# Pairing the attention pieces' y products in one PSUM bank, in a state-space and two-layer kernel ordered by a planner

## The chip, the cores and the metric

The kernel runs on one core of a Trainium2 chip. The metric is the device time of one execution in microseconds. The engines are called as in the profile: PE (TensorE; PEld is its weight load), DVE (VectorE), ACT (ScalarE), POOL (GpSimd), SP (SyncE, which issues most DMAs).

## The reference

A chunked state-space layer feeds two dense blocks. The layer has 4 batches, 8 heads, 768 steps, head size 32 and state size 16. Only this of it matters:

```python
for c in range(nc):
    L = np.exp(cum[:, :, :, None] - cum[:, :, None, :]) * causal
    M = np.einsum('bhin,bhjn->bhij', Cc, Bc) * L
    y[:, :, sl] = M @ xc + (Cc @ state) * decay_to_i
    state = decay_full * state + sum_j(Bx * decay_from_j)
x = y.transpose(0, 2, 1, 3).reshape(3072, 256)
h = x @ w_in;  g = h * sigmoid(1.702 * h);  x = g @ w_out
h = x @ w2_in; g = h * clip(h + 3, 0, 6) / 6;  out = g @ w2_out
```

Both dense blocks have width 256, inner width 2048 and 3072 tokens. All is fp32, and nearly fp32 accuracy is kept.

## The kernel before

**Order.** Every instruction group is added to a planner (class `Schedule`) with an engine, a guessed duration, a key (a due time) and the buffers that it reads, writes or takes anew. The planner simulates the engines, picks on each the earliest possible group and among equals the smallest key, and so fixes the order of each engine's queue before anything is built. Keys and guessed durations set only this order; on the chip the engines run their queues in order and wait on semaphores.

**Attention.** The layer is cut into 32 pieces q: 8 chunks of 96 steps, 4 batches each (`q = 4c + b`). A piece needs decay matrices `l:q` (two scans on DVE, line 425; for q of 6 and more the source is loaded by a DMA into one of 4 buffers), then S = B C products with the state columns appended (`s_mm`, line 460; from q = 6 on for two pieces at a time, in the banks `s`, `y` and two `acc`), then a multiplication of S by decay for each half of the heads (`g_mul` on DVE, line 463, or `g_copy` on ACT and `g_pool` on POOL, lines 466 and 470; `GMP` chooses), and then the y products (`y_mm`, line 481): 8 products of 112 rows by 32 columns, in the trace two records each. `YBANK(q)` puts even pieces in bank `y` and odd ones in bank `s`. ACT copies the new state out (`y_state`, line 485) and y as a rounded high half (`y_out`, line 495); DVE takes the low half (`y_lo`, line 498) and transposes the states of two batches (line 502) for the next chunk. `PIECE(q)` gives a piece's key.

**Dense blocks.** A fp32 product is made of three products of fp32r halves: high by low, high by high, low by high. The 3072 token columns are 6 blocks of 512. In the first dense block, blocks k = 0 to 3 go unit by unit (k, m), m = 0 to 15: 6 products of the first layer (`l1`, line 600), gelu on ACT (603), high half on ACT (612), low half on DVE or POOL (615; `GLP` chooses), and two units later 6 products of the second layer (`l2`, line 625). Blocks 4 and 5 and all of the second dense block (called A4, B0, B2, B4) go two blocks at a time with seven first-layer products in place of eight (`product`, line 761), whose parts ACT copies (`p_copy`, 770) and DVE adds (`p_add`, 773). Block k starts when all its columns are there; block 1 is columns 512 to 1023, pieces 5 to 10.

**Weights.** They come as 64-bit words and are unpacked (ACT line 332; ACT 337 or DVE 339, chosen by `LOW`), joined on DVE (343), rounded to a high half on ACT (346, `TOP`) and a low half on POOL (350). Weights 0 to 15 belong to the first dense block and are due unit by unit in block 0; 16 to 31 are decoded during A4 and B0.

**Outputs.** `outs` scales the sums of the second dense block by 1/6, half the features on ACT (line 778) and half on DVE (780), into one of 3 `gg` buffers, and SP stores each in two DMAs (783). The last sums are those of blocks 4 and 5.

Of the kernel before, what the change touches and what calls it, by code (L numbers as in the profile page):

```python
# [22 lines left out]
CH = 96  # L23
# [29 lines left out]
SKEY = lambda kind, i, lead, t: lead - 52 + 7 * i if i < NS_BX else t - 14  # L53
OPK = lambda kind, k, lead: [lead - 30 + 3.5 * i for i in range(7)] if kind == "A" else [lead - x for x in (22, 20, 18, 14, 9, 7, 5)]
GLQ = lambda kind, j: j == 1 or (kind == "B" and j == 0)
DECODE = (("A", 4), 14.0, 7.5)
# [8 lines left out]
def YBANK(q):  # L65
    return f"{'ys'[q % 2]}:y{q}"


PK = (48, 4, 88, 5, 114, 7, 156, 5)
UGAP = (4, 0.45)  # L70


def PIECE(q):
    if q < 6:
        return 6 + 2.2 * q + 3 * (q > 3)
    if q < 11:
        return PK[0] + PK[1] * (q - 6)
    if q < 16:
        return PK[2] + PK[3] * (q - 11)
    if q < 22:  # L80
        return PK[4] + PK[5] * (q - 16)
    return PK[6] + PK[7] * (q - 22)

# [140 lines left out]
def ssd_moe_kernel(ctx: ExitStack, tc: tile.TileContext, xs, aa, bc, bcz_d, bc0, wu, pat, idn, out):  # L224
# [247 lines left out]
    def y_view(q):  # L472
        return B_(YBANK(q))[:, 0:2 * E].rearrange("p (g e) -> p g e", g=2)

    def y_mm(q):
        c, b = divmod(q, NB)
        yv, x = y_view(q), B_(f"xs:{c}")
        for g in range(2):
            for k in range(4):
                h = 4 * g + k  # L480
                nc.tensor.matmul(out=yv[32 * k:32 * k + 32, g, :], lhsT=x[0:E, b, h * D:(h + 1) * D],  # L481
                                 rhs=B_(f"gm:{q}.{g}")[:, k, :], start=True, stop=True)

    def y_state(q):
        nc.scalar.copy(st_sb[:, q % NB, :, 0:NS], y_view(q)[:, :, CH:E])
# [8 lines left out]
    def y_out(q, k, a, b):  # L494
        nc.scalar.copy(x_part("h", q, k, a, b), y_view(q)[:, :, a:b])

    def y_lo(q, k, a, b):
        nc.vector.tensor_tensor(out=x_part("l", q, k, a, b), in0=y_view(q)[:, :, a:b], in1=x_part("h", q, k, a, b).bitcast(F32), op=ALU.subtract)
# [15 lines left out]
    for q in range(NC * NB):  # L514
# [40 lines left out]
        add("PE", 0.62, t + 2, y_mm, q, r=[f"gm:{q}.0", f"gm:{q}.1", f"xs:{c}"] + [f"xs:{c}.{b // 2}.{k}" for k in range(4) if c], new=[yn])  # L555
        if c + 1 < NC:
            add("ACT", 0.2, t + 2.1, y_state, q, r=[yn, "st_sb"], w=[f"st_sb{b}"])
        for k, a, e in block[q]:
            el = 0.1 + 0.0025 * (e - a)
            where = [f"bx:x{k}"] if k >= STD else [f"bx:{k}h", f"bx:{k}l"]  # L560
            if k not in taken:
                taken.add(k)
                for x in where:
                    sch.take(x, t + 2)
            add("ACT", el, t + 2.2, y_out, q, k, a, e, r=[yn, where[0]], w=[f"x{q}.{k}h"])
            if k < STD:
                add("DVE", el + 0.02, t + 2.3, y_lo, q, k, a, e, r=[yn, f"x{q}.{k}h", *where], w=[f"x{q}.{k}l"])
# [6 lines left out]
    def decode(p, k, after=0.0):  # L574
        R, Dn, W = f"bx:w{p}", f"dec:{p}", f"wt:{p}"
        add("SP", 0.4, k - 9, w_load, p, new=[R], kb=512, after=after)
        add("ACT", 0.72, k - 1.6, w_scale, p, r=[R], w=[f"hi{p}"])
        if LOW(p) == "ACT":
            add("ACT", 0.70, k - 1.5, w_low, p, True, r=[R], w=[f"low{p}"])
        else:  # L580
            add("DVE", 0.45, k - 1.9, w_low, p, False, r=[R], w=[f"low{p}"], port=True)
        add("DVE", 0.82, k - 1.0, w_join, p, r=[R, f"hi{p}", f"low{p}"], new=[Dn], port=True)
        e = TOP(p)
        add(e, {"ACT": 0.64, "DVE": 0.43, "POOL": 1.0}[e], k - 0.5, w_top, p, ENG[e], r=[Dn], new=[W])
        e = BOT(p)
        add(e, {"DVE": 0.78, "POOL": 1.46}[e], k, w_bottom, p, ENG[e], r=[Dn, W], w=[f"wl{p}"], port=True)
# [42 lines left out]
    def act_chain(kind, h, t, gh, gl, gp, off=False):  # L629

        src = f"gg:{h}" if (gp or off) and h[:2] != "hs" else h
        if kind == "A":
            add("ACT", 0.60, t, gelu, h, src, **({"w": [h]} if src == h else {"r": [h], "new": [src]}))
# [48 lines left out]
    def operands(kind, k, ks):  # L682
# [9 lines left out]
        def sub(v, a, b, new, key, r):  # L692
            e = TE(kind, v)
            add(e, 0.70 if e == "DVE" else 1.46, key, t_sub, ENG[e], fs[new], a, b, r=ready + r, **({"new": [pu[new]]} if new == v else {"w": [pu[new]]}), port=e == "DVE")

        def halves(v, s, key, r):
            add("ACT", 0.64, key, v_top, name[v], s, r=r, new=[name[v]])
            e = TE(kind, v)
            add(e, 0.70 if e == "DVE" else 1.46, key + 0.5, v_rest, name[v], s, ENG[e], r=[*r, name[v]], w=[name[v] + "l"], port=e == "DVE")
# [37 lines left out]
    def sums(kind, i, t):  # L737

        p0 = 2 * i + (NM if kind == "B" else 0)
        rcx, sf, sw = f"dec:s{i}", f"sf:{kind}{i}", sname(kind, i)  # L740
        e = SE(kind)
        pt = e == "DVE"
        if kind == "A":
            sch.take(rcx, t)
            for j in range(2):
                add(e, 0.43 if pt else 0.74, t + 0.1 * j, whole, rcx, p0 + j, ENG[e], r=[f"wt:{p0 + j}", f"wl{p0 + j}", rcx], w=[f"{rcx}.{j}"], port=pt)
            src = [rcx, f"{rcx}.0", f"{rcx}.1"]
        else:
            src = [f"dec:{p0}", f"dec:{p0 + 1}"]
        sch.take(sf, t + 0.2)  # L750
        for v in range(4):
            add(e, 0.29 if pt else 0.42, t + 0.2 + 0.1 * v, s_comb, sf, kind, i, v, ENG[e], r=src, w=[sf], port=pt)
        add("ACT", 0.64, t + 0.7, s_top, sw, sf, r=[sf], new=[sw])
        add(e, 0.70 if pt else 1.46, t + 0.8, s_rest, sw, sf, ENG[e], r=[sf, sw], w=[sw + "l"], port=pt)
# [20 lines left out]
    def o_scale(k, d, e):  # L775
        v = B_(f"gg:o{k}.{d}"), B_(f"acc:B{k}.{d}")
# [5 lines left out]
    def o_store(k, d, c, a, b):  # L782
        nc.sync.dma_start(out=out[c, d, :, a - T * c:b - T * c], in_=B_(f"gg:o{k}.{d}")[:, a - LO[k]:b - LO[k]])

    def outs(k, t):
        for d in range(2):
            e = ("ACT", "DVE")[d]
            add(e, 0.62, t, o_scale, k, d, e, r=[f"acc:B{k}.{d}"], new=[f"gg:o{k}.{d}"])
            a = LO[k]
            while a < LO[k + 1]:  # L790
                b = min(LO[k + 1], T * (a // T + 1))
                add("SP", 0.4, t + 0.5, o_store, k, d, a // T, a, b, r=[f"gg:o{k}.{d}"], w=[f"out{k}.{d}.{a}"], kb=(b - a) // 2)
                a = b

    nq = 0
    for si, (kind, k) in enumerate(sups):
        if (kind, k) == DECODE[0]:
            for p in range(NM, 2 * NM):
                td = lead[kind, k] + DECODE[1] + DECODE[2] * (p - NM)
# [4 lines left out]
        for i in range(NM // 2):  # L804
# [34 lines left out]
            if i == NM // 2 - 1:  # L839
                for half, tl in ((0, nxt + 6.3), (1, nxt + 8.9)):  # L840
# [64 lines left out]
```

## Time and profile before

| | us |
|---|---|
| median of 3 runs (581.56 to 585.34) | 581.97 |
| the profiled execution | 579.64 |
| its span, first to last instruction | 577.9 |
| PE busy in the span | 561.2 (97%) |
| DVE, ACT, POOL busy | 433.0, 343.7, 311.1 |
| mean granted TensorE clock, share of full speed | 0.992 |

Busy is what the profile counts as an instruction in progress. Products on PE overlap, so a busy PE can still be slower than its peak: the start of the next product tells more than the end of one.

### The profile page before, as it was taken

How to read it: one execution, taken by the hardware profiler on the slowest of the kernel's cores; microseconds unless marked ns; L12 is line 12 of the kernel's file. 1: busy time of each engine (PE TensorE's matmuls, PEld its weight loads, DVE VectorE, ACT ScalarE, POOL GpSimd, SP SyncE). 2: the span in 40 equal slices, each digit the busy share in tenths (PEclk: the TensorE clock that was granted, in tenths of full speed). 3: DMA queues.
4: the chain of work that ended last, by engine and by line, in shares of the span. 5: the costliest groups of instructions: out<-in, count | busy, mean ns of one | idle time of the engine just before them, and what ended most of it. 6: DMA issues, size and time to landing. Idle time of an engine off the chain costs nothing.

```text
span 577.9 us, 9020 instructions
## 1 busy us (share of the span) xinstructions
PE 561.2 (97%) x3292; PEld 448.5 (78%) x3292; DVE 433.0 (75%) x614; ACT 343.7 (59%) x652; POOL 311.1 (54%) x283
## 2 busy tenths in 40 slices
PE   8799989999999999999999999999999999999995
PEld 7587668777777777878888887888888888888884
DVE  6978997678676786588666798787777867777774
ACT  2888744445444546577877787656545655655542
POOL 3746366757344546568788777686222554322221
PEclk9799999999999999999999999999999999999999
DMA  8976421232424300331112310000200000200002
GB/s 177 371 174 199 112 90 25 83 105 63 111 59 109 112 2 1 127 129 37 36 38 73 111 36 1 1 2 0 72 2 1 0 2 0 74 0 1 0 1 73
DMA packets 21852, 37.72 MB, mean 65 GB/s; under 512 B 10528, under 2 KB 13968, under 8 KB 21808
## 3 DMA queue, kind: packets, MB, share of 16 engines
q1 hardware_dynamic: 20960, 36.79, 21.5%
q10 hardware_dynamic: 848, 0.35, 0.3%
q8 instruction: 26, 0.43, 0.3%
q14 instruction: 18, 0.15, 0.1%
HBM read 33.87 MB, written 3.26 MB: 64 GB/s over the span
## 4 chain that ended last, share of the span: by engine, by line
PE 91%; DVE 4%; DMA 2%; ACT 1%; issue 1%; POOL 0%; ACTq 0%; SPq 0%; DVEq 0%
PE acc L625 44%; PE h L761 18%; PE h L600 16%; PE s L761 4%; PE y L761 4%; PE s L460 2%; PE y L481 1%; PE s L481 1%; DMA bx_w<-in_wu 1%; DMA ov_a<-in_bcz 1%; DVE ov_b L773 1%; DVE dec L343 1%; PE h L460 1%; PE acc L600 0%; DVE ov_a L425 0%
## 5 line engine op out<-in xcount | busy, mean ns | idle before, releaser
L615 POOL TENSOR_TENSOR gl<-gg,gh 128x512 fp32r<-128x512 f32 x48 | 66.5, 1386 | 121.0 <-ACT gh L612 78.2
L625 PE MATMUL acc<-gh,wl 128*128 128x512 f32 x256 | 100.7, 393 | 0.0
L625 PE MATMUL acc<-gh,wh 128*128 128x512 f32 x256 | 100.1, 391 | 0.0
L425 DVE TENSOR_TENSOR_SCAN ov_a<-ov_a,pat_sb 112x448 f32<-112x448 f32 x52 | 76.5, 1498 | 9.0 <-DMA ov_a<-acl_d 8.9
L625 PE MATMUL acc<-gl,wh 128*128 128x512 f32 x256 | 80.3, 390 | 0.0
L625 PE MATMUL acc<-ov_b,wh 128*128 128x512 f32 x256 | 78.9, 390 | 0.0
L773 DVE TENSOR_TENSOR ov_b<-h,ov_b 128x512 f32<-128x512 f32 x64 | 44.0, 688 | 43.6 <-PE h L761 43.3
L615 POOL TENSOR_TENSOR ov_b<-ov_b 128x512 fp32r<-128x512 f32 x32 | 42.4, 1324 | 39.3 <-ACT ov_b L612 28.6
L612 ACT CAST gh<-gg 128x512 fp32r<-128x512 f32 x80 | 49.6, 620 | 21.3 <-DVE gg L609 20.6
L350 POOL TENSOR_TENSOR wl<-dec,wh 128x512 fp32r<-128x512 f32 x32 | 44.3, 1389 | 29.3 <-ACT wh L346 27.6
L625 PEld LDWEIGHTS acc<-gh,wl 128*128 128x128 f32 x256 | 48.1, 188 | 11.1 <-issue 0.9
L625 PEld LDWEIGHTS acc<-gl,wh 128*128 128x128 f32 x256 | 48.1, 188 | 10.2
L603 ACT ACTIVATE h<-h 128x512 f32<-128x512 f32 x46 | 26.8, 583 | 48.9 <-PE h L600 38.9
L625 PEld LDWEIGHTS acc<-ov_b,wh 128*128 128x128 f32 x256 | 48.1, 188 | 10.0
L625 PEld LDWEIGHTS acc<-gh,wh 128*128 128x128 f32 x256 | 48.1, 188 | 9.9
L606 ACT ACTIVATE gg<-h 128x512 f32<-128x512 f32 x48 | 28.7, 598 | 38.8 <-PE h L761 27.6
L615 DVE TENSOR_TENSOR gl<-h,gh 128x512 fp32r<-128x512 f32 x46 | 31.4, 683 | 24.8 <-ACT gh L612 23.8
L625 PE MATMUL acc<-ov_b,wl 128*128 128x512 f32 x128 | 49.9, 390 | 0.0
L470 POOL TENSOR_TENSOR ov_a<-ov_a 112x448 f32<-112x448 f32 x24 | 32.9, 1387 | 27.4 <-ACT ov_a L466 26.8
L603 ACT ACTIVATE gg<-h 128x512 f32<-128x512 f32 x32 | 19.1, 597 | 27.9 <-PE h L600 26.8
L609 DVE SCALAR_TENSOR_TENSOR gg<-gg,h 128x512 f32<-128x512 f32 x48 | 32.5, 678 | 1.4 <-ACT gg L606 1.1
L615 DVE TENSOR_TENSOR gl<-gg,gh 128x512 fp32r<-128x512 f32 x32 | 28.6, 895 | 4.9 <-ACT gh L612 4.7
(242 smaller groups left out, 1311.9 us busy)
## 6 DMA issues: line engine op xcount, KB each, us to landing
bx_w<-in_wu SPq DMA_DIRECT2D x32, 512.0 KB, 5.9
ov_a<-acl_d SPq DMA_DIRECT2D x26, 392.0 KB, 4.0
ov_a<-in_xs SPq DMA_DIRECT2D x8, 384.0 KB, 4.4
ov_a<-in_bc SPq DMA_DIRECT2D x96, 24.0 KB, 2.9
out<-gg SPq DMA_DIRECT2D x8, 192.0 KB, 1.9
out<-gg SPq DMA_DIRECT2D x8, 128.0 KB, 1.8
out<-gg SPq DMA_DIRECT2D x8, 64.0 KB, 1.6
ov_a<-in_bc SPq DMA_DIRECT2D x4, 112.0 KB, 6.4
```

Source lines behind the costliest of these rows:

```text
L350: e.tensor_tensor(out=lo, in0=B_(f"dec:{p}").bitcast(F32), in1=hi.bitcast(F32), op=ALU.subtract)
L425: nc.vector.tensor_tensor_scan(t, a, pat_sb, 0.0, ALU.mult, ALU.add)
L470: nc.gpsimd.tensor_tensor(out=t, in0=t, in1=B_(f"l:{q}")[:, 4 * g:4 * g + 4], op=ALU.mult)
L600: nc.tensor.matmul(out=B_(hn(u)), lhsT=w[:, 128 * j:128 * j + 128], rhs=x[:, j], start=x is xl and j == 0, stop=low and j == 1)
L603: nc.scalar.activation(B_(dst), B_(src), AF.Gelu_apprx_sigmoid)
L606: nc.scalar.activation(B_(dst), B_(src), AF.Relu, bias=3.0)
L609: nc.vector.scalar_tensor_tensor(out=B_(dst), in0=B_(g), scalar=6.0, in1=B_(h), op0=ALU.min, op1=ALU.mult)
L612: nc.scalar.copy(B_(dst), B_(src))
L615: e.tensor_tensor(out=B_(dst), in0=B_(src), in1=B_(hi).bitcast(F32), op=ALU.subtract)
L625: nc.tensor.matmul(out=B_(acc[d]), lhsT=w[:, 256 + 128 * d:384 + 128 * d], rhs=g, start=first and d not in seen, stop=last and d not in [v ...
L761: nc.tensor.matmul(out=B_(dst), lhsT=w, rhs=x, start=start and i == 0, stop=i == 2, skip_group_check=True)
L773: nc.vector.tensor_tensor(out=B_(dst), in0=B_(a), in1=B_(b), op=ALU.add)
```

## The change

Seven edits, of which the diff below is the core.

1. From piece 6 on the y products of an even piece and the next odd one are one run (`y_mm(pieces)`), due with the odd one, into one bank (448 of its 512 columns); banks `y` and `s` take turns by pairs. Where both pieces lie in one block, the state copy, the high half and the low half are one instruction for the two; the state copy always is.
2. `PIECE` gives other keys: pieces 6 to 11 are one group from 46.3 on, in steps of 4; before it was 6 to 10 from 48 on, and piece 11 at 88. The gap between units in the plan begins at unit 8, not 4.
3. The last two blocks' outputs go into `pu` buffers (7 of them, by then free), and the very last scaling is cut into a left half on ACT, stored from ACT's queue, and a right half on DVE, stored from SP's.
4. `TOP`: the high halves of weights 3, 7, 28, 30, 31 go to POOL. `LOW`: weights 8, 16 to 22 on DVE (before 16 to 21).
5. `GMP`: pieces over 21 (before 15) have one S multiplication on POOL. `GLP`: in block 1 all low halves go to POOL, in block 2 every second, in block 3 every fourth (before: every second in all three). `GLQ`: other choices in B0, B2 and B4, as many as before.
6. Other keys for sums, operands, decoding, and for the gelu chains and second-layer products of A and B (`TH`, `TL`: second-layer products due 0.9 to 3.6 later).
7. Some guessed durations; `PKEY` is not used.

```diff
-TOP = lambda p: "ACT"
+TOPP = (3, 7, 28, 30, 31)
+TOP = lambda p: "POOL" if p in TOPP else "ACT"
-LOW = lambda p: "ACT" if p < NM or p >= 22 else "DVE"
-GMP = lambda q, g: (g == 1 and (q in (0, 1, 2, 3, 4, 6) or q > 15)) or (q, g) in ((3, 0), (4, 0))
-GLP = lambda kind, k, m: k > 0 and m % 2 == 0
+LOWD = (8, 16, 17, 18, 19, 20, 21, 22)
+LOW = lambda p: "DVE" if p in LOWD else "ACT"
+GMP = lambda q, g: (g == 1 and (q in (0, 1, 2, 3, 4, 6) or q > GM1)) or (q, g) in ((3, 0), (4, 0))
+GM1 = 21
+GLP = lambda kind, k, m: m % 4 in GLM[k]
+GLM = ((), (0, 1, 2, 3), (1, 3), (0,))
-GLQ = lambda kind, j: j == 1 or (kind == "B" and j == 0)
+GQ = {'A4': (1,), 'B0': (1, 2), 'B2': (1, 3), 'B4': (0, 3)}
+TH = (3.3, 5.7, 8.6, 9.0)
+TL = (3.3, 6.5, 8.4, 12.4)
...
-    return f"{'ys'[q % 2]}:y{q}"
-PK = (48, 4, 88, 5, 114, 7, 156, 5)
-UGAP = (4, 0.45)
+    return f"{'ys'[q % 2]}:y{q}" if q < 6 else f"{'ys'[q // 2 % 2]}:y{q // 2 * 2}"
+PK = (46.3, 4.0, 91, 5.6, 116.3, 6.7, 151.7, 5.1)
+UGAP = (8, 0.45)
...
+    i = (q >= 12) + (q >= 16) + (q >= 22)
+    return PK[2 * i] + PK[2 * i + 1] * (q - (6, 12, 16, 22)[i])
...
+        i = 2 * E * (q % 2) if q >= 6 else 0
+        return B_(YBANK(q))[:, i:i + 2 * E].rearrange("p (g e) -> p g e", g=2)
+    def y_mm(pieces):
+        for q in pieces:
+            c, b = divmod(q, NB)
...
-        add("PE", 0.62, t + 2, y_mm, q, r=[f"gm:{q}.0", f"gm:{q}.1", f"xs:{c}"] + [...], new=[yn])
+        pieces = (q,) if q < 6 else (q - 1, q)
+        if q < 6 or q % 2:
+            add("PE", 0.62 if q < 6 else 1.0, t + 2, y_mm, pieces, r=[f"gm:{i}.{g}" for i in pieces for g in range(2)] + [...], new=[yn])
+            jobs = [(i, k, a, e, False) for i in pieces for k, a, e in block[i]]
+            if q >= 6 and len(jobs) == 2 and jobs[0][1] == jobs[1][1]:
+                jobs = [(q - 1, jobs[0][1], 0, CH, True)]
...
+    def o_name(k, d):
+        return f"{'pu' if k >= NB6 - 2 else 'gg'}:o{k}.{d}"
...
+            end = k == NB6 - 1 and d == 1
+            for f, g, e in ((0, BW // 2, "ACT"), (BW // 2, BW, "DVE")) if end else ((0, BW, ("ACT", "DVE")[d]),):
...
+                    q = "ACT" if end and f == 0 else "SP"
```

## Rows read from the trace of the kernel before

**Rows 1.** Busy time of each engine by stage of the kernel, first line: the columns.

```profile
core 0: us, PE busy (x) PEld busy (x) DVE busy (x) ACT busy (x) POOL busy (x), PEclk, DMA share, GB/s
...
44.00:81.60 37.60, 34.75 (x295) 25.41 (x293) 34.74 (x51) 25.81 (x55) 20.33 (x15) 1.00 0.47 140
81.60:130.00 48.40, 48.40 (x357) 37.39 (x355) 35.98 (x54) 23.32 (x48) 32.70 (x38) 1.00 0.27 73
...
232.00:312.00 80.00, 78.68 (x347) 64.53 (x346) 56.75 (x77) 58.85 (x107) 58.41 (x62) 1.00 0.20 66
312.00:395.00 83.00, 82.58 (x363) 67.81 (x362) 64.46 (x92) 58.23 (x105) 62.58 (x56) 1.00 0.12 39
```

**Rows 2.** Chain of work around one y run: start us, us, what.

```profile
98.08 1.36 PE acc L625 x6
99.44 0.52 PE s L481 x16
99.96 1.60 PE h L600 x6
101.56 1.38 PE acc L625 x6
```

**Rows 3.** The y products, line 481: duration ns min/median/max, first and last start.

```profile
L481 PE MATMUL y<-ov_a x256: 258/259/394, 10.4 to 219.1; 112*32 112x112 f32 x128
```

**Rows 4.** Timeline of DVE before block 1: start us, us, instruction.

```profile
66.72 1.96 DVE L425 TENSOR_TENSOR_SCAN ov_a<-ov_a,pat_sb 112x448 f32<-112x448 f32 x1
...
68.92 1.08 DVE L425 TENSOR_TENSOR_SCAN ov_a<-ov_a,pat_sb 112x448 f32<-112x448 f32 x1
...
80.36 0.26 DVE L498 TENSOR_TENSOR bx_1l<-y,bx_1h 128x128 fp32r<-128x128 f32 x1
...
80.68 1.25 DVE L425 TENSOR_TENSOR_SCAN ov_a<-ov_a,pat_sb 112x448 f32<-112x448 f32 x1
...
82.43 1.14 DVE L463 TENSOR_TENSOR ov_a<-acc,ov_a 112x448 f32<-112x448 f32 x2
```

**Rows 5.** Timeline of PE at the same place, the wait in brackets.

```profile
78.01 0.73 PE L600 MATMUL h<-bx_0l,wh 128*128 128x512 f32 x2 [1.74 <-ACT wh L346]
...
79.13 0.59 PE L481 MATMUL y<-ov_a 112*32 112x112 f32 x16
...
81.60 0.62 PE L600 MATMUL h<-bx_1l,wh 128*128 128x512 f32 x2
```

**Rows 6.** Timeline near 354 us, ACT and PE.

```profile
351.73 0.62 ACT L346 CAST wh<-dec 128x512 fp32r<-128x512 f32 x1
...
353.73 0.58 ACT L770 COPY ov_b<-h 128x512 f32<-128x512 f32 x1
...
354.37 0.74 PE L761 MATMUL h<-bx_B21B,wh 128*128 128x512 f32 x2 [0.35 <-ACT ov_b L770]
```

**Rows 7.** Timeline of the tail, and line 783's DMA issues (ns min/median/max).

```profile
569.64 0.60 ACT L778 ACTIVATE gg<-acc 128x512 f32<-128x512 f32 x1 [1.75 <-PE acc L625]
...
570.96 0.62 PE L625 MATMUL acc<-ov_b,wh 128*128 128x512 f32 x2
570.98 4.36 SPq L783 DMA_DIRECT2D out<-gg  x8
573.81 0.69 DVE L780 TENSOR_SCALAR gg<-acc 128x512 f32<-128x512 f32 x1 [2.86 <-DMA out<-gg]
...
L783 SPq DMA_DIRECT2D out<-gg x24: 332/411/452, 411.8 to 574.9; - x24
```

**Rows 8.** Scans (line 425), POOL's low halves (L615), unpack on DVE (L339).

```profile
L425 DVE TENSOR_TENSOR_SCAN ov_a<-ov_a,pat_sb x52: 1057/1183/3207, 34.6 to 211.3; 112x448 f32<-112x448 f32 x52
...
L425 DVE TENSOR_TENSOR_SCAN ov_a<-acc,pat_sb x12: 1064/1078/1092, 5.3 to 22.4; 112x448 f32<-112x448 f32 x12
...
L615 POOL TENSOR_TENSOR gl<-gg,gh 128x512 fp32r<-128x512 f32 x48 | 66.5, 1386 | 121.0 <-ACT gh L612 78.2 <-PE h L761 42.8
...
L339 DVE TENSOR_SCALAR bx_w<-bx_w 128x512 uint32<-128x512 uint32 x6 | 3.8, 634 | 1.5 <-DMA bx_w<-in_wu 1.5
```

More of the change, by code (lines that the diff above doesn't have):

```diff
@@ L472, in y_view, with y_two, y_state @@
     def y_view(q):
[L473 to L485, printed above, removed]
+        i = 2 * E * (q % 2) if q >= 6 else 0
+        return B_(YBANK(q))[:, i:i + 2 * E].rearrange("p (g e) -> p g e", g=2)
+    def y_two(q):
+        return B_(YBANK(q))[:, 0:4 * E].rearrange("p (i g e) -> p g i e", i=2, g=2)
+    def y_mm(pieces):
+        for q in pieces:
+            c, b = divmod(q, NB)
+            yv, x = y_view(q), B_(f"xs:{c}")
+            for g in range(2):
+                for k in range(4):
+                    h = 4 * g + k
+                    nc.tensor.matmul(out=yv[32 * k:32 * k + 32, g, :], lhsT=x[0:E, b, h * D:(h + 1) * D],
+                                     rhs=B_(f"gm:{q}.{g}")[:, k, :], start=True, stop=True)
+    def y_state(q, pair):
+        if pair:
+            b = q % NB
+            nc.scalar.copy(st_sb[:, b:b + 2, :, 0:NS].rearrange("p i g e -> p g i e"), y_two(q)[:, :, :, CH:E])
+        else:
+            nc.scalar.copy(st_sb[:, q % NB, :, 0:NS], y_view(q)[:, :, CH:E])
     def x_raw(n):
@@ L554, in ssd_moe_kernel @@
         yn = YBANK(q)
[L555 to L567, printed above, removed]
+        pieces = (q,) if q < 6 else (q - 1, q)
+        if q < 6 or q % 2:
+            add("PE", 0.62 if q < 6 else 1.0, t + 2, y_mm, pieces, r=[f"gm:{i}.{g}" for i in pieces for g in range(2)] + [f"xs:{c}"] + [f"xs:{c}.{b // 2}.{k}" for k in range(4) if c], new=[yn])
+            if c + 1 < NC:
+                add("ACT", 0.2 if q < 6 else 0.24, t + 2.1, y_state, pieces[0], q >= 6, r=[yn, "st_sb"], w=[f"st_sb{i % NB}" for i in pieces])
+            jobs = [(i, k, a, e, False) for i in pieces for k, a, e in block[i]]
+            if q >= 6 and len(jobs) == 2 and jobs[0][1] == jobs[1][1]:
+                jobs = [(q - 1, jobs[0][1], 0, CH, True)]
+            for i, k, a, e, pair in jobs:
+                el = 0.1 + 0.0025 * (e - a) * (1 + pair)
+                where = [f"bx:x{k}"] if k >= STD else [f"bx:{k}h", f"bx:{k}l"]
+                if k not in taken:
+                    taken.add(k)
+                    for x in where:
+                        sch.take(x, t + 2)
+                xn = [f"x{j}.{k}" for j in ((i, i + 1) if pair else (i,))]
+                add("ACT", el, t + 2.2, y_out, i, k, a, e, pair, r=[yn, where[0]], w=[x + "h" for x in xn])
+                if k < STD:
+                    add("DVE", el + 0.02, t + 2.3, y_lo, i, k, a, e, pair, r=[yn, *[x + "h" for x in xn], *where], w=[x + "l" for x in xn])
         if b % 2 and c + 1 < NC:
@@ L637, in act_chain @@
             add("DVE", 0.70, t + 0.5, hard, h, g, src, r=[h, g], w=[src], port=h[:2] == "hs")
-        add("ACT", 0.62, t + 1.0, top, src, gh, r=[src], new=[gh])
+        add("ACT", 0.61, t + 1.0, top, src, gh, r=[src], new=[gh])
         e = "POOL" if gp else "DVE"
-        add(e, 1.46 if gp else 0.70, t + 1.5, rest, src, gh, gl, ENG[e], r=[src, gh], new=[gl], port=not gp and src[:2] in ("gg", "hs"))
+        add(e, 1.33 if gp else 0.70, t + 1.5, rest, src, gh, gl, ENG[e], r=[src, gh], new=[gl], port=not gp and src[:2] in ("gg", "hs"))
     parts = {k: [f"x{q}.{k}{v}" for q in block for kk, a, b in block[q] if kk == k for v in ("hl" if k < STD else "h")] for k in range(NB6)}
@@ L693, in sub @@
             e = TE(kind, v)
-            add(e, 0.70 if e == "DVE" else 1.46, key, t_sub, ENG[e], fs[new], a, b, r=ready + r, **({"new": [pu[new]]} if new == v else {"w": [pu[new]]}), port=e == "DVE")
+            add(e, 0.70 if e == "DVE" else 1.33, key, t_sub, ENG[e], fs[new], a, b, r=ready + r, **({"new": [pu[new]]} if new == v else {"w": [pu[new]]}), port=e == "DVE")
         def halves(v, s, key, r):
```

91 lines of the change are left out of this document (48 added, 43 removed).

## The prediction

> **What bounds the kernel now.** I read the page first: PE is busy 97% of the span, and the chain of work that ended last is PE for 91%. That says "TensorE bound" but not where anything is left, so I cut the span into the kernel's own stages [rows 1]. The reader is to compare PE's busy time with the length of each stage. It is full from 81.6 to 232 us (three rows, one shown) and from 395 to the last product (two more rows, at most 0.02 us idle). Four places are left: the head up to 26.8 us; 44 to 81.6 us, where PE misses 2.85 us and where DVE is busy 34.7 of 37.6 us; 232 to 395 us, where PE misses 1.32 + 0.42 us; and what follows the last product. A full PE is not an efficient one, so next I looked at the chain for what a y run costs [rows 2], then at DVE and PE around 80 us [rows 4, 5], at one stall behind ACT near 354 us [rows 6], and at the tail [rows 7].
>
> **Part 1: two pieces' y products in one run.** Six big products take 1.36 us when nothing is between them. After a y run the next six take 1.60 and the six after that 1.38 [rows 2]: so a run costs its own 0.52 us plus 0.24 + 0.02 for the change over, 0.78 in all. There are 512 such records, 256 in each of two like rows, at 16 to a run: 32 runs, of which pieces 6 to 31 have 26 [rows 3], each standing alone between big products. The change makes 13 runs of 32 out of them. The 0.52 us is per product and stays; the change over is paid 13 times less: at most 13 x 0.26 = 3.4 us, and 13 x 0.21 = 2.7 us if the small slowdown some products later belongs to the run's length. I take 3.1 us, near the upper end, since the 1.60 us row shows nearly all of it directly behind the run. Nearly all of it lies where PE is full, so it shortens the path one for one. If a long run paid per product what a short one pays per change over, it would be nothing: that is a rival below.
>
> The copies behind the run (state copy, output copy, low half on DVE) also become fewer, and ten of the thirteen pairs have both pieces in one 512-column block and get one copy for two. ACT and DVE have spare time in every stage but one, so I cost this at nothing; in that one stage it saves DVE two short instructions, which I leave out.
>
> **Part 2: the pair must be complete.** A y run now waits for all four products of S and decay, and piece 11 must be ready with piece 10. Unit column block 1 needs piece 10 but not piece 11. Before, piece 10's run starts at 79.13, its low half ends at 80.62 and block 1's first product starts at 81.60 without a wait [rows 4, 5]; piece 11's two scans and two multiplications on DVE come only then, and end at 82.43 + 1.14 = 83.57. So I expect the changed kernel's pair (10, 11) to be bound by DVE. With DVE's order kept: run from 83.6 for 1.04 us, the low half done 0.97 us after its end (before: from 79.13 + 0.52 to 80.62), block 1 at 85.6, that is 4.0 us late. PE can fill 1.36 us of this with the second-layer products of block 0's last unit, which are due at that point anyway, and 0.1 us is the extra run less the change overs saved. That leaves 2.5 us lost. But the new keys place pieces 6 to 11 from 46.3 instead of 48, and DVE has 2.9 us idle in this stage [rows 1]; if half of that is filled, 1.4 us comes back. The unpack of weight 8 moves from ACT to DVE, 0.63 us [rows 8], which takes part of that again. Ends: 2.85 us gained (every stall of PE here gone) and 3.9 us lost (order kept, nothing filled). I take 1.2 us lost.
>
> **Part 3: the last outputs.** The fourth scaling starts at 573.81 although the last product pair started at 570.96 and ended 0.62 us later; it waited 2.86 us for its buffer, which a store still read [rows 7]. With buffers of its own it can start near 571.65, and a half takes some 0.35 us, half of 0.69. But then SyncE's queue is late next: eight stores are issued there in a row, each 0.33 to 0.45 us, the last at 574.9 [rows 7]. Six of them, issued from 570.98 with no wait for the buffer, keep the queue busy until about 573.8, and the right half's store is the seventh. So the last issue moves from 574.9 to 573.8, and it is smaller: 1.25 us gained. The left half's two stores go out on ACT's queue from about 572.1 and end earlier than that. Ends: 0.5 us (if the second queue disturbs the first) and 1.95 us (if the stores whose scaling ended at 570.24 go first, the queue starts 0.7 us earlier). I take 1.25.
>
> **Part 4: who does the helpers.** The roundings of weights 3, 7, 28, 30 and 31 move from ACT to POOL. Near 354 us a product waits 0.35 us for ACT's copy of V, which stands in ACT's queue behind such a rounding of 0.62 us [rows 6]; the three late ones fall in that stretch, so that stall should go. At most all 1.74 us of idle PE between 232 and 395 go [rows 1]; but the keys of the second-layer products, operands and sums all change there too, and one new stall of the kind seen costs 0.5 to 1 us. Bounds: 1.7 us gained, 2 us lost; I take 0.5 gained, nearest to the one stall whose cause is seen. Block 1's low halves all go to POOL (8 more), block 2 keeps 8, block 3 drops from 8 to 4, and six S multiplications come back to DVE: two POOL instructions fewer in all, at 1.39 us each [rows 8]. PE is full from 81.6 to 232 us with DVE at 36.0 of 48.4 us [rows 1], so the moves are covered there; without that cover each late low half would cost what it is late. The new durations in the table of costs and the unused key list issue nothing.
>
> **Sum.** -3.1 + 1.2 - 1.25 - 0.5 = -3.65 us. Against the profiled execution (579.64 us, of which the span is 577.9) that is 576.0; that execution was 2.3 us under the median of the runs shown. Against the median: 581.97 - 3.65 = 578.3 us.
>
> **A rule weighed.** The scans from SBUF take 1.06 to 3.21 us, the same scans from PSUM never over 1.09 [rows 8]: something on the SBUF side stretches them, up to threefold. The Trainium skill, "SBUF — State Buffer", section "Who interferes with whom", says that a VectorE operation with two SBUF inputs and a GpSimd operation that reads SBUF exclude each other for a whole instruction. The trace agrees as far as two lengths of one shape go. By that rule the moves to POOL of roundings 3 and 7 and of the low halves would speak against this change; what they would do in the one stage that is short of DVE is the second rival.
>
> **The rivals.** *(a) The stage at 44 to 81.6 us clears.* The new order fills DVE's idle time, weights 14 and 15 are no longer decoded behind scans (PE waits 1.74 us for one at 78.01 [rows 5]), and the late stalls go. For it: 2.9 us of idle DVE, and a wait whose cause is only an order. Against it: the work of piece 11 comes in. Time: -3.4 - 1.25 - 1.4 (half of PE's idle time here) - 1.7 = -7.75, so 574.2 us.
>
> *(b) Slower: pair (10, 11) is held by blocked scans.* Place: DVE from 60 to 84 us. The scans of pieces 8 to 11 are eight; single ones took 1.08 and 1.96 [rows 4]. If POOL's work meets each of them, they take 0.7 us more each, 5.6 us on DVE with no idle time filled. Then block 1 starts near 91 us, PE loses 4.0 + 5.6 - 0.1 - 1.36 = 8.1 us, and the sum is -3.1 - 1.25 + 8.1 - 0.5 = +3.3: 585.2 us. It decides from block 1's first product at about 88 us. For it: DVE has only 8% to spare there. Against it: POOL's work in that stage hardly grows.
>
> *(c) A run of 32 saves nothing.* The second piece loads other weights and writes other columns of the bank, and could pay the change over again. Against it: 16 products already take other weights each at a steady 0.03 us. Time: +1.2 - 1.25 - 0.5 = -0.55, so 581.4 us.
>
> **How the numbers follow.** Forecast 0.50 (alone 576 to 580.5), (a) 0.28, (b) 0.10, (c) 0.12. One per cent is 5.8 us, about what a measurement of this kernel can tell from no change. Faster by more needs under 576.15: most of (a), 0.24, and a low end of the forecast, 0.06: 0.30. Slower by more needs over 587.8: a third of (b), 0.03. The rest is 0.67. The range reaches into (a) to 572.8 and over (c) to 581.9, leaving out (b) and the low end of (a).
>
> **What would show it.** Right: 13 y runs of 32 records after piece 5, each about 1.05 us, with one pair of 1.60 and 1.38 behind it; block 1's first product between 82 and 86 us, with DVE full before it and PE idle in front; the last four scalings without a wait for a store, and the last issue near 2.2 us after the last product instead of 3.3; no wait of PE on ACT's copy of V near 354 us. Wrong: a 32-record run above 1.3 us or followed by slow products throughout (c); block 1 before 81 us (a) or after 88 us (b); new idle PE between 81.6 and 232 us, which would mean that POOL holds back low halves; a head longer than 26.8 us, which I leave unchanged because pieces 0 to 5 are.

## The result: 1.4% faster, and where the time went

| | before | after |
|---|---|---|
| median (range) of 6 runs each | 583.65 (581.42 to 585.62) | 575.48 us (572.82 to 577.58) |
| the profiled execution, its span | 579.64, 577.9 | 577.55, 575.8 us |
| mean granted TensorE clock in it | 0.992 | 0.978 |

The ratio is 0.9859, 95% interval 0.9811 to 0.9908. Against the 578.3 us of the forecast the time is 2.8 us shorter; it lies within the range of 572.8 to 581.9, and just below the 576 us where the likeliest case ended. One thing has to be known to read any number here: the time of either kernel goes with the mean granted clock of the execution (the mean takes all stretches at half clock together, wherever they lie), so I compare at like clock. Over all its runs, those beside the experiments included, before took 585.1 to 586.1 us at 0.977 to 0.978 and 581.0 to 581.9 at 0.989, with others between, below (at 0.992) and above (at 0.976); after took 577.2 to 577.6 at 0.978 and 572.8 to 573.7 at 0.989 to 0.990. That is 8 us less at either clock. The two profiled executions are not at like clock, and their spans, 2.1 us apart, hide most of it.

The stages, first by windows of the trace of after, cut as in [rows 1], with block 1's first product at 88.79 us (columns as there: the stretch, its length, busy time and instructions of PE, PEld, DVE, ACT and POOL, PEclk, DMA share, GB/s); ahead of them two stretches of the head:

```profile
13.00:21.00 8.00, 7.73 (x74) 6.02 (x74) 6.00 (x12) 3.65 (x10) 3.58 (x4) 0.59 0.99 328
21.00:33.00 12.00, 9.49 (x87) 6.70 (x87) 9.59 (x18) 8.74 (x22) 9.53 (x8) 0.50 1.04 367
...
44.00:88.79 44.79, 41.74 (x336) 32.16 (x334) 39.17 (x62) 28.72 (x57) 22.42 (x21) 0.96 0.43 128
88.79:130.00 41.21, 41.21 (x290) 33.13 (x290) 32.02 (x36) 18.83 (x34) 30.56 (x24) 1.00 0.22 67
232.00:312.00 80.00, 79.90 (x353) 65.82 (x352) 59.16 (x80) 57.68 (x105) 58.64 (x63) 1.00 0.20 66
312.00:395.00 83.00, 82.82 (x365) 67.94 (x364) 63.58 (x95) 58.48 (x107) 62.62 (x60) 1.00 0.12 39
```

The same two stretches of the head in the trace of before:

```profile
13.00:21.00 8.00, 7.25 (x118) 5.75 (x120) 7.30 (x13) 5.43 (x16) 5.53 (x5) 1.00 1.00 334
21.00:33.00 12.00, 8.76 (x62) 6.02 (x60) 10.23 (x19) 9.95 (x23) 7.82 (x8) 0.72 1.03 353
```

Read the PEclk column, the third from the right, first. In this execution of after TensorE ran at half clock (0.50, 1.2 GHz) through most of the head, in that of before only in part of it. Block 0's first product comes at 30.37 us instead of 26.79: 3.6 us that are no work of the change. From 232 to 395 us PE now misses 0.10 + 0.18 us instead of 1.32 + 0.42: 1.5 us gained. And the stage before block 1, which ended at 81.60, ends at 88.79; counted from block 0's first product it is 58.4 us instead of 54.8, with a clock of 0.96. Part of that is order: six second-layer products of block 0 (1.36 us) and piece 11's half of the run now stand ahead of block 1's first product.

The chain of work of after around one y run (start us, us, what), to be held against [rows 2]:

```profile
113.34 1.36 PE acc L654 x6
114.70 0.90 PE y L492 x32
115.60 1.58 PE h L629 x6
117.19 1.36 PE acc L654 x6
```

Two pieces took 2 x (0.52 + 0.24 + 0.02) = 1.56 us; one run of 32 with its change over takes 0.90 + 0.22 = 1.12 us. All 13 runs of after have 32 records and nearly this length where nothing is waited for, so the merge gave 13 x 0.44 = 5.7 us. The six products behind the run are as slow as before (1.58), the six after them are no longer slow at all.

PE before block 1 in after (timeline, waits in brackets):

```profile
74.56 0.73 PE L629 MATMUL h<-bx_0l,wh 128*128 128x512 f32 x2 [1.45 <-ACT wh L352]
...
81.47 0.72 PE L629 MATMUL h<-bx_0l,wh 128*128 128x512 f32 x2 [1.43 <-ACT wh L352]
...
82.83 1.22 PE L629 MATMUL h<-bx_0h,wl 128*128 128x512 f32 x2 [0.17 <-POOL wl L356]
83.85 0.63 PE L654 MATMUL acc<-gh,wl 128*128 128x512 f32 x1
84.28 0.63 PE L654 MATMUL acc<-gh,wh 128*128 128x512 f32 x1
...
86.39 0.97 PE L492 MATMUL s<-ov_a 112*32 112x112 f32 x32
...
88.79 0.64 PE L629 MATMUL h<-bx_1l,wh 128*128 128x512 f32 x2
```

and DVE at the same place:

```profile
72.20 1.07 DVE L431 TENSOR_TENSOR_SCAN ov_a<-ov_a,pat_sb 112x448 f32<-112x448 f32 x1
73.19 0.66 DVE L349 SCALAR_TENSOR_TENSOR dec<-bx_w 128x512 uint32<-128x512 uint32 x1
...
75.44 2.86 DVE L431 TENSOR_TENSOR_SCAN ov_a<-ov_a,pat_sb 112x448 f32<-112x448 f32 x2
78.22 0.53 DVE L521 TENSOR_TENSOR bx_1l<-y,bx_1h 128x384 fp32r<-128x384 f32 x1
78.78 1.26 DVE L525 STREAM_TRANSPOSE ov_a<-st_sb 32x128 f32<-32x128 f32 x4
80.07 0.69 DVE L349 SCALAR_TENSOR_TENSOR dec<-bx_w 128x512 uint32<-128x512 uint32 x1
...
84.78 1.12 DVE L469 TENSOR_TENSOR ov_a<-acc,ov_a 112x448 f32<-112x448 f32 x2
```

The wait of 1.74 us in [rows 5] is there twice. Each time PE waits for ACT's rounding of a weight, and ACT's rounding has to wait for DVE's join of it (L349), which stands in DVE's queue behind scans and transposes: the join at 73.19 frees the product at 74.56, that at 80.07 the one at 81.47. After these pauses the starts of products are 0.43 us apart (83.85, 84.28) where they are 0.227 apart elsewhere: TensorE at 1.2 GHz again, for eight products of block 0, the pair at 82.83 included. The pair (10, 11) runs at 86.39 without a wait of its own; DVE's last multiplications for piece 11 (84.78) end half a microsecond earlier, at 85.90.

The tail of after (timeline), against [rows 7]:

```profile
569.91 3.28 SPq L815 DMA_DIRECT2D out<-ov_b  x7
570.55 0.42 DVE L812 TENSOR_SCALAR ov_b<-acc 128x256 f32<-128x256 f32 x1 [0.67 <-PE acc L654]
571.01 0.38 ACT L810 ACTIVATE ov_b<-acc 128x256 f32<-128x256 f32 x1 [0.54 <-DVE ov_b L812]
571.42 0.88 ACTq L815 DMA_DIRECT2D out<-ov_b  x2
```

The 2.86 us wait for a store is gone. Seven issues take 3.28 us on SP's queue where eight took 4.36. From the start of the last product pair to the end of the kernel it is 5.86 us instead of 6.90: 1.0 us gained. The ACT half, meant to run beside the DVE half, waited for it.

So the profiled executions add up: -5.7 (merge), +0.2 (idle PE before block 1: 3.05 us instead of 2.85), -1.5 (stalls from 232 to 395 us) and -1.0 (tail) make -8.0 us, which is what the runs are apart at like clock. Twelve more products of block 0 at half clock, 0.2 us each (four at its start, eight before block 1), add 2.4, and the head adds 3.6: -2.0, beside the -2.1 of the spans. What is uncertain in this is whose the clock's 6.0 us are. The last two groups of runs below bear on that.

### The profile page after: what moved, and what is told of

It reads as the page before. It is cut to its first block, busy times and chain, and to the rows that moved or that the text cites. A ratio compares the mean times of both kernels' runs of the same rounds, so it can differ in the third digit from the quotient of the medians.

```text
span 575.8 us, 8953 instructions
## 1 busy us (share of the span) xinstructions
PE 562.3 (98%) x3292; PEld 455.0 (79%) x3292; DVE 426.9 (74%) x612; ACT 335.0 (58%) x619; POOL 310.4 (54%) x286
## 4 chain that ended last, share of the span: by engine, by line
PE 92%; DVE 3%; issue 2%; POOL 1%; DMA 0%; ACT 0%; ACTq 0%; POOLq 0%; DVEq 0%
PE acc L654 45%; PE h L790 19%; PE h L629 15%; PE s L790 4%; PE y L790 4%; PE s L466 2%; PE s L492 1%; PE y L492 1%; POOL ov_a L476 1%; DVE ov_a L431 1%; PE acc L421 1%; PE h L466 1%; DVE ov_a L469 1%; PE acc L629 0%; DVE dec L349 0%
## 5 line engine op out<-in xcount | busy, mean ns | idle before, releaser
L644 POOL TENSOR_TENSOR gl<-gg,gh 128x512 fp32r<-128x512 f32 x44 | 64.9, 1479 | 71.2 <-ACT gh L641 36.3
L431 DVE TENSOR_TENSOR_SCAN ov_a<-ov_a,pat_sb 112x448 f32<-112x448 f32 x52 | 74.2, 1459 | 7.7 <-DMA ov_a<-acl_d 7.5
L644 POOL TENSOR_TENSOR ov_b<-ov_b 128x512 fp32r<-128x512 f32 x24 | 31.4, 1308 | 50.6 <-ACT ov_b L641 31.8
L654 PEld LDWEIGHTS acc<-gl,wh 128*128 128x128 f32 x256 | 48.3, 189 | 10.2
L644 DVE TENSOR_TENSOR gl<-h,gh 128x512 fp32r<-128x512 f32 x58 | 39.6, 682 | 20.7 <-ACT gh L641 20.5
L635 ACT ACTIVATE gg<-h 128x512 f32<-128x512 f32 x48 | 28.7, 598 | 42.8 <-PE h L790 36.6
L641 ACT CAST gh<-gg 128x512 fp32r<-128x512 f32 x68 | 42.2, 621 | 17.0 <-DVE gg L638 12.1
L632 ACT ACTIVATE h<-h 128x512 f32<-128x512 f32 x42 | 24.4, 582 | 43.5 <-PE h L629 37.1
L644 POOL TENSOR_TENSOR ov_b<-gg,ov_b 128x512 fp32r<-128x512 f32 x16 | 21.1, 1317 | 42.7 <-ACT ov_b L641 30.7
L641 ACT CAST gh<-h 128x512 fp32r<-128x512 f32 x58 | 34.1, 588 | 14.2 <-DVE h L638 12.5
L632 ACT ACTIVATE gg<-h 128x512 f32<-128x512 f32 x36 | 21.5, 597 | 35.1 <-PE h L629 31.3
L476 POOL TENSOR_TENSOR ov_a<-ov_a 112x448 f32<-112x448 f32 x18 | 23.5, 1322 | 25.9 <-ACT ov_a L472 25.7
```

The source lines that it names most:

```text
L431: nc.vector.tensor_tensor_scan(t, a, pat_sb, 0.0, ALU.mult, ALU.add)
L476: nc.gpsimd.tensor_tensor(out=t, in0=t, in1=B_(f"l:{q}")[:, 4 * g:4 * g + 4], op=ALU.mult)
L632: nc.scalar.activation(B_(dst), B_(src), AF.Gelu_apprx_sigmoid)
L635: nc.scalar.activation(B_(dst), B_(src), AF.Relu, bias=3.0)
L641: nc.scalar.copy(B_(dst), B_(src))
L644: e.tensor_tensor(out=B_(dst), in0=B_(src), in1=B_(hi).bitcast(F32), op=ALU.subtract)
```

## The experiments

**Is the saving the change over, or the products?** The first kernel keeps the plan of after and splits each run: the second piece's 16 records are issued one group of products later.

```diff
     for o in ops:
+        if o["fn"] is y_mm and len(o["args"][0]) == 2:
+            y_mm(o["args"][0][:1])
+            held = o
+            continue
...
+        if held is not None and o["eng"] == "PE":
+            y_mm(held["args"][0][1:])
+            held = None
```

> The planned order of the changed kernel is kept; only the second piece's eight y products are issued one PE group later, so that the 13 long runs become 26 short ones again. Theory A (the gain is change overs on PE that are no longer paid): 26 runs of 0.73 us in place of 13 of 1.11, with the slower products behind them some 0.43 us for each pair, so 5 to 6 us above the changed kernel, that is 580.5 to 581.5 us. Theory B (the gain comes from the new order and the new helpers): within 1 us of the changed kernel, 574.5 to 576.5 us.

583.75 us, ratio to before 0.9996 (0.996 to 1.0032): the whole gain is gone. At like clock it is 7.8 us above after (581.0 against 573.2 us at 0.989), more than expected. The chain of this kernel shows the two change overs again:

```profile
113.38 0.52 PE y L492 x16
113.90 1.14 PE h L629 x4
115.05 0.52 PE y L492 x16
115.56 0.66 PE h L629 x2
116.23 1.37 PE acc L654 x6
```

Four products take 1.14 us instead of 0.91, two 0.66 instead of 0.45, and each run pays its 0.52: 0.37 us more for the pair than one run of 32, or 4.8 us for 13. The rest is mostly in new waits before block 1, since a held piece is late. Its list of PE's waits (total us, times, longest) has

```profile
PE h L629 <- ACT wh L352: 4.1, 3, 1.5
...
PE h L629 <- DVE bx_1l L521: 1.3, 1, 1.3
```

where after has 2.9 us and none: 2.5 us. Those belong to this way of splitting; the price of the change overs is the 4.8 us.

**What does a record cost inside a run?** The second kernel issues the 16 products of each long run twice (the same values are written twice).

```diff
-        for q in pieces:
+        for q in pieces * (len(pieces)):
```

> Each long run issues its 16 y products twice, 64 records in place of 32, with the same result. If a record in a long run costs 0.024 us, as 0.904 less 0.521 us for 16 more of them says: 13 x 0.77 = 10 us above the changed kernel, 585.5 us. If it costs 0.0325 us, as the prediction took it: 13.5 us above, 589 us. If PE were not the bound around these runs (theory B): under 5 us above.

584.22 us, ratio 1.0018 (0.9985 to 1.0052). One run of it in the chain:

```profile
111.05 1.67 PE y L492 x64
112.72 1.58 PE h L629 x6
114.31 1.36 PE acc L654 x6
```

32 more records cost 1.67 - 0.90 = 0.77 us, 0.024 each, and the products behind are as slow as behind 32. So 16 records are 0.385 us of the 0.52, and 0.135 us of a run is paid once, however long it is, beside the 0.22 to 0.26 us in the products behind it. The Trainium skill, "TensorEngine Tiling (Array Packing)", section "Tiling Modes", says that a change of tiling mode drains the engine, without a price; the records of 112 rows by 32 columns between 128 by 128 agree with it as far as a price per run goes, and these are the price here. The total rose 8.5 us at like clock, not 13 x 0.77 = 10.0. The traces account for it: from block 0's first product to the last product of the kernel it is 547.75 us instead of 539.75, with 0.3 us less idle PE and only 4.2 us at half clock instead of 8.0 (half of the difference, 1.9 us, is time); without these two it is 10.2 us more.

**Alone.** Two kernels add parts of the change to before: the pairs only, with the old keys; and the pairs with the new keys of the pieces and of the gap between units.

```diff
-PK = (48, 4, 88, 5, 114, 7, 156, 5)
-UGAP = (4, 0.45)
+PK = (46.3, 4.0, 91, 5.6, 116.3, 6.7, 151.7, 5.1)
+UGAP = (8, 0.45)
```

> The kernel before with the runs, banks and copies in pairs alone: old keys (piece 11 due at 88), old helpers, old outputs. Theory A: 13 runs of 1.1 us, 5.6 us less on PE, but block 1 waits for piece 11 and starts 59 to 63 us after block 0's first product, in place of 54.8, which gives back 3 to 7 us: 578 to 585 us. Theory B: no gain from pairing, 583 us or more, with y runs that do not change the sum of PE's work.

> The kernel before with the pairs and with the new keys of the pieces and units (piece 11 due with pieces 6 to 10); old helpers, other keys and outputs. Theory A: the sum of y runs as in the changed kernel (13.0 us beside the big products), block 1 some 58 us after block 0's first product; the late waits (0.94, 0.85 us and less) and the tail as before, so 2 to 3 us above the changed kernel: 577.5 to 579 us over both of its levels. Theory B (helpers and other keys carry the gain): 580 us or more, like the pairs alone.

580.79 us, 0.9942 (0.9908 to 0.9977), and 579.36 us, 0.9922 (0.9887 to 0.9958). At 0.988 to 0.99 the steps are 581.5, 578.5, 576.45 and 573.2 us for before, pairs, pairs with keys, and after: 3 us by the pairs, 2 by the keys, 3.2 by all else. The pairs give only 3 of their 5.7 us when the keys are old: block 1 then comes 61.2 us after block 0 instead of 54.8, and from 44 to 130 us PE is idle for 5.23 us instead of 2.85. The second time lies 0.4 us above the expected range.

**The helpers.** After, with the old choice of engines for roundings, unpacks, S multiplications and low halves.

```diff
-TOPP = (3, 7, 28, 30, 31)
+TOPP = ()
-LOWD = (8, 16, 17, 18, 19, 20, 21, 22)
+LOWD = (16, 17, 18, 19, 20, 21)
-GM1 = 21
+GM1 = 15
-GLM = ((), (0, 1, 2, 3), (1, 3), (0,))
+GLM = ((), (0, 2), (0, 2), (0, 2))
-GQ = {'A4': (1,), 'B0': (1, 2), 'B2': (1, 3), 'B4': (0, 3)}
+GQ = {'A4': (1,), 'B0': (0, 1), 'B2': (0, 1), 'B4': (0, 1)}
```

> The changed kernel with the old choice of engines (roundings all on ACT, unpack, S multiplications and low halves as before), everything else new, planned anew. Theory A: the late waits come back (some 1 to 2 us), the rest stays: 576.5 to 578 us. Theory B: most of the 8 us goes, 580 us or more.

581.21 us, 0.9958 (0.9917 to 1.0): some 4 us lost at like clock (577.0 to 578.0 near 0.989, 581.2 to 581.9 at 0.978), more than the late waits that theory A names and half of the 8 us. Its waits of PE show from where:

```profile
PE h L629 <- ACT wh L352: 3.6, 3, 1.9
...
PE h L790 <- DVE ov_b L802: 0.8, 1, 0.8
PE h L629 <- ACT gg L632: 0.7, 1, 0.7
...
PE h L629 <- DVE bx_1l L521: 0.3, 1, 0.3
```

After has 2.9 us for the first, 0.2 for the second and none for the other two. These four make 2.3 us; no single one carries the loss, and the rest has no place that the waits show. The late roundings alone were tried in one more kernel (28, 30 and 31 back on ACT).

```diff
-TOPP = (3, 7, 28, 30, 31)
+TOPP = (3, 7)
```

> The changed kernel with the roundings of weights 28, 30 and 31 on ACT again. If those three cause the wait near 354 us: a wait of PE on ACT's copy of V comes back there, 0.3 to 0.9 us in all. If the new keys removed it: PE's waits between 312 and 395 us stay under 0.6 us together, as in the changed kernel.

Its one time is 573.52 us at a clock of 0.987, as after, and PE has no wait on ACT's copy of V. The kernel with all the old engines has none either; with the pairs and the pieces' keys alone it is there, 0.36 us at 353.27. So the stall of [rows 6] did not go because those roundings moved; the other new keys keep it away.

**The tail.** After, with the last scalings in `gg` buffers and uncut, as before.

```diff
-        return f"{'pu' if k >= NB6 - 2 else 'gg'}:o{k}.{d}"
+        return f"{'gg'}:o{k}.{d}"
...
-            end = k == NB6 - 1 and d == 1
+            end = False
```

> The changed kernel with the old outputs: gg buffers, the last scaling whole on DVE, all stores from SyncE. Theory A: the last scaling waits for a store again, and from the last product to the end it takes 6.6 us in place of 5.6: 1 us longer, all else alike to 0.3 us. If the tail's gain lay elsewhere (an earlier last product), less than 0.5 us.

From the start of the last product pair to the end it is 6.83 us, 0.97 more than after; the wait is back:

```profile
569.72 4.36 SPq L815 DMA_DIRECT2D out<-gg  x8
572.55 0.69 DVE L812 TENSOR_SCALAR gg<-acc 128x512 f32<-128x512 f32 x1 [2.86 <-DMA out<-gg]
```

The one time (578.32 us, at 0.977) says the same: 0.7 to 1.1 us above after at that clock.

**What limits the stage before block 1?** Two suspects: the pair (10, 11), which makes piece 10 wait for piece 11, and the joins. Three kernels: pieces 10 and 11 with runs and banks of their own; the weights from 12 on due 7 us earlier; both.

```diff
-        pieces = (q,) if q < 6 else (q - 1, q)
-        if q < 6 or q % 2:
+        pieces = (q,) if ONE(q) else (q - 1, q)
+        if ONE(q) or q % 2:
...
-        decode(p, tu[p] - 1.5, WAFTER[p] if p < len(WAFTER) else 0.0)
+        decode(p, tu[p] - 1.5 - EARLY * (12 <= p), WAFTER[p] if p < len(WAFTER) else 0.0)
```

> Pieces 10 and 11 have runs and banks of their own again, so block 1 need not wait for piece 11; all else as in the changed kernel, planned anew. Theory A: block 1's first product comes 54 to 56 us after block 0's first, in place of 58.4, one change over more (0.43 us); 1 to 3 us under the changed kernel, 572.5 to 574.5 us. If DVE's work before block 1 bounds that stage whatever the pair waits for: block 1 at 58 us again and the time within 1 us of the changed kernel.

577.29 us, 0.9878 (0.9813 to 0.9943). Block 1 comes 1.9 us earlier after block 0, but the time is that of after at either clock: piece 11's run and six second-layer products now follow block 1's first product instead of preceding it, and from 44 to 130 us PE is idle for 3.03 us, in after 3.05. Alone, the pair is not what the stage waits for.

> The kernel after with the weights from piece 12 on due 7 us earlier and nothing else; the pair of pieces 10 and 11 stays. Theory A (the joins of the weights in VectorE's queue set block 1, the pair doesn't): like the variant that also gives the two pieces runs of their own, 573.1 give or take 1, the waits on L352 gone from 68 to 85 us. Theory B (the pair, held by the blocked scans, is what remains once the joins are early): 1 to 3 us slower than that variant, 574 to 576, with a wait of TensorE on the y products' operands before the run of pieces 10 and 11.

575.54 us, 0.988 (0.9823 to 0.9937): no gain either. The waits on L352 are gone, and the pair is late in their place; PE is idle for 3.71 us from 44 to 130. PE in this kernel:

```profile
82.17 0.59 PE L492 MATMUL s<-ov_a 112*32 112x112 f32 x16
85.53 0.93 PE L492 MATMUL s<-ov_a 112*32 112x112 f32 x16 [2.77 <-DVE ov_a L469]
```

and DVE:

```profile
82.15 2.81 DVE L431 TENSOR_TENSOR_SCAN ov_a<-ov_a,pat_sb 112x448 f32<-112x448 f32 x2
84.88 1.12 DVE L469 TENSOR_TENSOR ov_a<-acc,ov_a 112x448 f32<-112x448 f32 x2
```

Piece 10's half of the run is done, then the run stands for 2.77 us until piece 11's two scans (2.81) and the first of its multiplications are through.

> The changed kernel with own runs for pieces 10 and 11 and with weights 12 to 15 due 7 us earlier. If PE's two waits of 1.6 and 1.8 us and the low clock behind them come from weights whose join stands behind scans in DVE's queue: both go, 3 to 5 us less than the changed kernel: 571 to 572.5 us over both levels. If DVE is simply full before block 1: the waits move to the y runs and the time stays within 1 us of the changed kernel.

Both together: 573.07 us, 0.9806 (0.9762 to 0.9849), its four runs from 571.69 to 575.54. (The two waits that the expectation names are those of 1.45 and 1.43 us.) Block 1 comes 52.7 us after block 0. The waits stand one behind the other: the earlier joins alone hand the time to the pair, and only with both edits does the idle time of PE from 44 to 130 us fall, to 2.49 us. That is 0.6 us, and the additional run costs 0.4 of it. More lies in the clock: in this execution it stays at 1.00 before block 1, where after lost 1.6 us. So the waits themselves are worth little; that the clock stays up for want of them is argued from single traces.

**Whose is the clock?** After, with 26 small products added in the pauses of the head, so that PE is not idle there (their results are overwritten).

```diff
-        for i in range(2):
+        for i in (0, 1) * (1 + (q == 3)):
...
+        if q in FILL:
+            add("PE", 0.15 * FILL[q], t + 1.9, fill, yn, FILL[q], r=["gh:acl", "al", "sel"], new=[yn])
...
+        if not u:
+            add("PE", 0.15 * FILL0, t - 0.1, fill, h, FILL0, r=["gh:acl", "al", "sel"], new=[h])
```

> The changed kernel with idle PE time in the head filled: the row spreads of piece 3 issued twice, 4 and 6 extra products ahead of the y runs of pieces 4 and 5, and 8 ahead of block 0's first product; their results are overwritten. If the two levels of the time come from TensorE's clock in the head (0.5 from 14 us on in one, from 21 us on in the other): most executions at the upper level of the granted clock, median 572 to 573.5 us. If the levels come from elsewhere: both levels again, 575 to 577 us.

572.34 us, 0.9785 (0.9741 to 0.983). Its four runs lie between 571.23 and 573.4 us, at 0.992 to 0.995; none is near 577 us, as three of after's six are. So those are made in the head, by TensorE's clock, and it is worth some 4 us. Last, all three edits together:

> The kernel after with what the two faster variants did, together: pieces 10 and 11 with runs and banks of their own and the weights from piece 12 on due 7 us earlier, and the 26 small products that keep TensorE busy in the head. Theory A (two separate losses, the clock in the head and the waits on the joins before block 1): about 570 us, 569 to 571.5, below both variants (573.1 and 572.3), all runs at the upper level, block 1 starting 50 to 53 us after block 0 and within 81 us of the start. Theory B (one loss: both variants only bring the head's clock up): no better than the one with the filled head, 571.5 to 573.

569.99 us (569.75 to 570.77), ratio 0.9773 (0.9726 to 0.9821), the best of all: 5.5 us under the median of after. The windows of its trace, from the head to block 1's first product:

```profile
13.00:21.00 8.00, 8.00 (x124) 6.44 (x126) 7.25 (x13) 5.39 (x16) 5.56 (x5) 1.00 1.00 337
21.00:33.00 12.00, 9.92 (x81) 7.76 (x79) 11.69 (x20) 11.28 (x25) 9.78 (x9) 1.00 1.02 370
33.00:44.00 11.00, 11.00 (x50) 9.09 (x49) 8.08 (x12) 9.46 (x18) 7.30 (x6) 1.00 0.68 179
44.00:78.11 34.11, 32.28 (x289) 24.50 (x287) 33.19 (x50) 22.75 (x46) 23.45 (x20) 1.00 0.39 121
```

PEclk is 1.00 throughout, and the stage is 51.35 us long from block 0's first product, 7 us less than in after and 3.5 less than before. As above this is clock and order more than idle time, which is 2.52 us from 44 to 130 and 2.88 with the filled head alone. That kernel's trace still has the clock at half from 26.5 to 29.9 us and from 77.7 to 81.1, together 6.7 us of PE's work at half speed or some 3.3 us of time; the medians are 2.35 us apart. DVE is busy 33.19 of 34.11 us in the last window, and PE's wait of 0.92 us at its end is for DVE: now DVE is the bound of the stage.

## Why the prediction was right and where it was off

**Part 1, the merge: right mechanism, term too small.** 3.1 us stood against 5.7. The step that failed is "The 0.52 us is per product and stays". The doubled runs show 0.024 us a record, so only 0.385 of it stays, and 0.135 us is paid per run. Per pair that is 0.26 us for the change over saved (the upper end of my bounds), 0.14 for the run's own price (2 x 0.52 - 0.90) and 0.04 because the change over that stays takes 0.22, not 0.26: 13 x 0.44 = 5.7 us. The row for a 32-record run was forecast at 1.05 us and came at 0.90. The rival that a long run saves nothing (c) is out: the chain shows one price for 32 records, and the split runs pay 4.8 us again.

**Part 2, the stage before block 1: near, for the wrong reason.** Forecast 1.2 us lost; after lost 0.2 us in idle PE and, in the profiled execution, 1.6 us in eight products at half clock, 1.8 in all; the forecast had no clock in it. The step that failed: I let DVE's work for piece 11 set block 1, at 82 to 86 us. In after that work is no wait at all, though by only half a microsecond. PE waits twice for weights whose joins stand behind DVE's scans, the same cause as the 1.74 us of [rows 5], which I had read and then left for rival (a) instead of carrying it through the new order. The mechanism I described is real: it appears, at 2.77 us, as soon as the joins are early. Rival (b) priced it at 8.1 us and let block 1 decide from 88 us on. That mark was passed (88.79) only because the head was late: in the run with the late roundings on ACT, whose block 0 starts at 26.6, block 1 starts at 84.8 us.

**Part 3, the tail: right.** Forecast 1.25, measured 1.04 by the profile and 0.97 by the undone edit. The last issue on SP's queue starts 2.85 us after the last product pair instead of 3.94, 1.1 us sooner, as forecast. The rest of the 1.25 was for that store being smaller, and it is not: the right half's store went out fifth of the seven, and the last is again one of 192 KB, which lands 1.99 us after its issue (before 1.95). The ACT half, though it waited 0.54 us for the DVE half, costs nothing here: its stores have landed 0.8 us before the last one.

**Part 4, helpers and keys: too small, and partly the wrong cause.** Forecast 0.5 us gained; PE's idle time from 232 to 395 us fell by 1.46, and the helpers are worth some 4 us in the end, the keys of the pieces 2. The stall of [rows 6] did go, but not because of the roundings that I named. It is also the smallest of three: most of the 1.46 us are two waits of before for DVE's additions, which I had counted and not looked into.

```profile
247.08 0.73 PE L761 MATMUL h<-bx_T4A,wh 128*128 128x512 f32 x2 [0.78 <-DVE ov_b L773]
...
254.04 0.96 PE L761 MATMUL h<-bx_T3A,bx_SA 128*128 128x512 f32 x3 [0.54 <-DVE ov_b L773]
```

With the old engines the first is back (0.79 us), the second is not. I had called the moves to POOL covered in both directions; undoing them costs small waits in four places. What POOL's new work did to the scans shows in the row of after that answers to [rows 8]:

```profile
L431 DVE TENSOR_TENSOR_SCAN ov_a<-ov_a,pat_sb x52: 1056/1206/2179, 41.5 to 211.3; 112x448 f32<-112x448 f32 x52
```

The median is much as it was (1183 ns before), the longest is shorter (before 3207). But POOL's work as a whole did not grow: 310.4 us busy, 311.1 before. The rule of the Trainium skill that I weighed ("SBUF — State Buffer", section "Who interferes with whom") was not put to the test by that; scans of 1056 and 2179 ns of one shape still agree with it.

**The sum.** Measured -8.0 us without the clock and -5.6 with the slow products of block 0 in the profiled executions, against -3.65. Rival (a) came nearest in time (574.2), by another road: it had the merge at 3.4 and the stage cleared, where the stage did not clear and the merge was 5.7. "Within 1%" got 0.67, and the kernel is 1.4% faster. Narrow bounds on the merge (2.7 to 3.4) made that chance too high: they came from one chain of rows and supposed that a run has no price of its own. The head, which I left unchanged, came 3.6 us later in the profiled execution of after; it was a sign of being wrong in the forecast, and the other profiles show that the clock makes it, not the change: kernels with the change and a clock that fell later have block 0 at 26.4 to 26.8 us.

## What to carry to other kernels

Small products between big ones cost a price per run as well as per product: take it from two run lengths before estimating a merge, not from one. In a stage that lacks one engine's time, list every wait that this engine's queue can cause in order; removing the first can hand its time to the second. The start of a stage can move by order alone: count the idle time and the clock, too. Compare executions at like granted clock, and look whether a pause in the head has thrown the clock down before reading a difference of under 1% as work.

## What the runs showed of the hardware that was not expected

TensorE's clock in the head decides 4 us. In after PE waited for ACT near 12 us,

```profile
13.27 1.03 PE L466 MATMUL h<-ov_a 16*112 16x112 f32 x14 [1.00 <-ACT ov_a L472]
```

and from 14.5 us on its clock was 0.50; before waited at the same place,

```profile
13.29 1.03 PE L460 MATMUL h<-ov_a 16*112 16x112 f32 x14 [0.81 <-ACT ov_a L466]
```

and kept 1.00 until 22.9 us. This wait alone does not make the difference: in the kernel with pieces 10 and 11 apart it was 0.81 us too, and the clock fell at 14.4 us. What does was not found. But in all fourteen profiles block 0's first product comes at 26.4 to 26.8 us where the clock fell after 20 us or not at all, and at 28.9 to 30.5 us where it fell between 14 and 16. Filling the pauses of the head kept the clock up in nine runs of two kernels, all at 0.992 or higher.

Before block 1 two waits of 1.4 us, 7 us apart, stood ahead of the same fall: after them eight big products ran at half clock. It is so in all five profiled kernels that have this pair of waits (after, the one with pieces 10 and 11 apart, the old tail, the late roundings back on ACT, the filled head). But the kernel with split runs waits 1.50 and 1.40 us there and its clock stays at 1.00, so these waits alone do not decide it either. In the kernel with all three edits waits of 0.20 and 0.92 us are left at that place, and the clock stays at 1.00.
